# Decode attention over 65,536 keys: whole key tiles at the head, two value tiles in one run of TensorE's loop, and another order of the last pieces

## The chip, the cores and the metric

The kernel runs on one core of a Trainium2 chip. The metric is device time in microseconds (us), the median of repeated executions. A profile is one further execution, recorded by the hardware profiler: it has a time of its own, and a span from the first to the last recorded instruction. All times inside the profile count from the start of that span.

## What is computed

One decode step of attention with grouped heads: 32 query heads share 8 key/value heads, so each of the 8 groups has 4 queries, 65,536 keys and as many values of 128 numbers, in bf16.

```python
B, Hq, Hkv, Sq, Sk, D = 1, 32, 8, 1, 65536, 128
scores = jnp.einsum("bhqd,bhkd->bhqk", q, k) * scale     # k, v repeated 4 times over heads
p = _softmax(scores, axis=-1)
return jnp.einsum("bhqk,bhkd->bhqd", p, v)
```

Keys and values are 16 MiB for each group, 268.4 MB for the eight groups together. Each byte is read once.

## The kernel before

**Tiles.** A tile is half of one group's keys or values: 256 rows in each of 128 partitions, 64 KB a partition, 8 MiB in all. A tile is called k or v with its group and half: k00 is the first half of the keys of group 0, v71 the second half of the values of group 7. The on-chip buffer `buf` is a ring of three tiles. SyncE issues all loads on one queue, in a fixed order: k00, k01, k10, k11, v00, then for each group g from 2 to 7 the tiles kg0, kg1, v(g-2)1, v(g-1)0, and at the end v61, v70, v71 (line 153). With more than three tiles, the load of a tile waits until the tile three places earlier in the list has been used, because it goes into the same place of the ring (lines 158 to 169). For k10, k20, and the first halves of keys in general, that is told by `clr`, the count of cleared score banks: the place of a first half of keys is free once the third bank of its group has been cleared, since the first two banks are then done. The place of a second half of keys is free by `kb`, which VectorE raises when the group's four banks are closed. The place of a value tile is free by `vit`, raised by TensorE after every 32 rows.

So the load of k11 (fourth in the list) waits for the third bank of group 0, that of v00 for `kb` of group 0, that of k20 (sixth) for the third bank of group 1, that of k21 for `kb` of group 1, and that of v01 for the values v00.

**Landing.** A load raises its semaphore by 16 when all of it has landed. The tiles of group 0, and those of the last key group, are loaded as two transfers of 128 rows; their halves have the semaphores `sK[b][0]` and `sK[b][1]` of the ring's place b. The key tiles between are one transfer that raises `sK[b][0]` alone; for them ScalarE raises `sK[b][1]` ahead of time with three counts, in the first turn of its loop (lines 254 to 258). The value tiles v60, v61 and v70 are loaded in parts (`BY`), v71 in eight pieces (`PIECES`, of 64, 64, 32, 32, 44, 8, 8 and 4 rows).

**Keys.** VectorE transposes a landed half tile in place, one instruction of 128x8192 words (`turn`, line 312), and raises `kt`. For each half tile TensorE clears a score bank (`clr`), runs 32 matmuls into it and closes it (blocks "bank" to "bank_end"). A group has four half tiles and four banks. Then VectorE takes the maximum, TensorE spreads it ("summed"), ScalarE takes the exponentials of all four banks, and VectorE transposes the weights (`weights`).

**Values.** TensorE's block "values" handles 32 rows a turn, 8 matmuls, once `sV` says that they have landed; for the last four value tiles GpSimd passes the landings on to `sV` (lines 215 to 220). `r_w` is the column of the weights, `r_e` where the run ends. A run ends in "values_done", from where TensorE goes on to "turn" (the next group's keys, or "late", which sets the end of the next run), to "summed" or to "tail". In groups 0 to 7 a run is one value tile. VectorE's `picked` reduces a finished sum, TensorE's `chosen` gathers it.

**The end.** In block "tail" TensorE multiplies the piece of 44 rows with 11 matmuls, closes the bank, multiplies the last 8, 8 and 4 rows one by one into another bank, waits for VectorE's `picked` (`mxs`), adds it by `chosen`, and ScalarE scales and stores the result.

The lines that the prediction's steps touch most:

```python
140    first = load(0, kr[0], 0, 0, NT // 2)
164                sp.wait_ge(*((kb, wh + 1) if ws else (clr, 4 * wh + 3)))
314        for x in range(2):
315            take(dve, sK[b][x], 16)
318            dve.transpose(out=kv, in_=kv).then_inc(kt, 1)
450        take(pe, kt)
451        clear(sc[:, ds(value(r_x, 4) * 512, 512)]).then_inc(clr, 1)
```

Of the kernel before, what the change touches and what calls it, by code (L numbers as in the profile page):

```python
# [9 lines left out]
ALU = mybir.AluOpType  # L10
# [3 lines left out]
G = 8  # L14
H = 4
P = 128
D = 128
NT = 256
# [1 line left out]
C = 16  # L20
SLIDE = P + 4 * (W - 1)
BY = {
    (G - 2, 0): (128, 128), (G - 2, 1): (128, 128), (G - 1, 0): (128, 64, 64),
}
N = 2
FAR = 2.0 ** 126
STEP = 32
PIECES = (64, 64, 32, 32, 44, 8, 8, 4)
MOVED = 4


# [1 line left out]
def kernel(  # L33
# [18 lines left out]
    _, Hkv, Sk, _ = k.shape  # L52
# [5 lines left out]
    pe, dve, act, pool, sp = nc.tensor, nc.vector, nc.scalar, nc.gpsimd, nc.sync  # L58
# [16 lines left out]
    o_r = sbuf("o_r", (P, D + 3))  # L75
# [6 lines left out]
    sel = sbuf("sel", (P, H))  # L82
# [9 lines left out]
    misc = psum("misc", (P, 512))  # L92
# [7 lines left out]
    sK = [[sem(f"sK{b}{x}") for x in range(2)] for b in range(3)]  # L100
# [11 lines left out]
    wqs = sem("wqs")  # L112
    cst = sem("cst")
    mxs = sem("mxs")
# [5 lines left out]
    outs = sem("outs")  # L120
    rls = sem("rls")
    end = sem("end")
    dl = sem("dl")
    pl = sem("pl")
    cleared = list(sems)
# [3 lines left out]
    kr = [k[0, g].rearrange("(p n) d -> p (n d)", p=P) for g in range(G)]  # L129
    vr = [v[0, g].rearrange("(p n) d -> p (n d)", p=P) for g in range(G)]  # L130

    def load(at, src, s, lo=0, n=NT):
        at = at % 3 * half + lo * D
        return sp.dma_start(  # L134
            out=buf[:, at:at + n * D], in_=src[:, s * half + lo * D:s * half + (lo + n) * D]
        )

    first = load(0, kr[0], 0, 0, NT // 2)  # L140
    tc.no_tile_sem_insts.add(first.ins.name)
    first.then_inc(sK[0][0], 16)
    tc.add_to_no_dep_group("first", first.ins)
# [3 lines left out]
    tc.compile()  # L147


    load(0, kr[0], 0, NT // 2, NT // 2).then_inc(sK[0][1], 16)  # L150
    load(1, kr[0], 1, 0, NT // 2).then_inc(sK[1][0], 16)
    load(1, kr[0], 1, NT // 2, NT // 2).then_inc(sK[1][1], 16)
    tiles = [("k", 0, 0), ("k", 0, 1), ("k", 1, 0), ("k", 1, 1), ("v", 0, 0)]
    for g in range(2, G):
        tiles += [("k", g, 0), ("k", g, 1), ("v", g - 2, 1), ("v", g - 1, 0)]
# [2 lines left out]
    for at, (kind, h, s) in enumerate(tiles):  # L158
        if at < 2:
            continue  # L160
        if at > 2:
            was, wh, ws = tiles[at - 3]
            if was == "k":
                sp.wait_ge(*((kb, wh + 1) if ws else (clr, 4 * wh + 3)))
            else:

                if (wh, ws) not in BY:
                    sp.wait_ge((sC, sD)[ws], 16 * (wh + 1)).then_inc(sV, NT // STEP)
                sp.wait_ge(vit, NT // STEP * (2 * wh + ws + 1))
        if kind == "k" and h == G - 1:  # L170
            for x in range(2):
                load(at, kr[h], s, x * NT // 2, NT // 2).then_inc(sK[at % 3][x], 16)
        elif kind == "k":
            load(at, kr[h], s).then_inc(sK[at % 3][0], 16)
        elif (h, s) == (G - 1, 1):
            lo = 0
            for n, land in zip(PIECES, sP):
                load(at, vr[h], s, lo, n).then_inc(land, 16)
                lo += n
        elif (h, s) in BY:  # L180
            lo = 0
            for n in BY[h, s]:
                load(at, vr[h], s, lo, n).then_inc(lands.pop(0), 16)
                lo += n
        else:
            load(at, vr[h], s).then_inc((sC, sD)[s], 16)
# [7 lines left out]
        out=ident[:, :], in_=ident[:, :], compare_op=ALU.not_equal, fill=1.0,  # L194
# [8 lines left out]
    for g in range(G):  # L203
        if g == 0:
            pool.wait_ge(qxs, 1)
        else:
            pool.wait_ge(outs, g)
        pool.tensor_tensor(  # L208
            out=wv[:, :, :, 0:H],
# [6 lines left out]
    for at, (land, n) in enumerate(list(zip(sL, sum(BY.values(), ()))) + list(zip(sP, PIECES))[:MOVED]):  # L216

        pool.wait_ge(land, 32 if land is sP[0] else 16).then_inc(sV, n // STEP)
        if at + 1 == len(BY[G - 2, 0]):
            pool.wait_ge(outs, G).then_inc(wqs, 2)  # L220

    def take(engine, semaphore, n=1):

        engine.wait_ge(semaphore, n).then_inc(semaphore, -n)  # L224


    act.dma_start(out=qn, in_=q[0, :, 0, :]).then_inc(sQ, 16)
    act.wait_ge(qps, 1)
    act.copy(
        out=qx[:, :].rearrange("p (b r h) -> p b h r", b=2, r=2),  # L230
# [10 lines left out]
    for g in range(G + 1):  # L241
        if g < G:
            act.wait_ge(nms, g + 1)
            act.activation(  # L244
                out=E[:, :], in_=sc[:, :], func=ACT.Exp, bias=nmb[:, 0:1], scale=SCALE,
                accum_out=o_r[:, D:D + 1],
            ).then_inc(exd, 1)

        act.wait_ge(rls, g + 1)
        at = max(g - 1, 0) * D  # L250
        act.activation(  # L251
            out=o_out[:, at:at + D], in_=psum_f[0:H, 0:D], func=ACT.Copy, scale=rl
        ).then_inc(outs, 1)
        if g == 0:

            for b in range(3):
                n = sum(kind == "k" and at % 3 == b and 0 < h < G - 1 for at, (kind, h, _) in enumerate(tiles))
                act.nop().then_inc(sK[b][1], 16 * n)
    act.wait_ge(outs, G + 1)
    store(1, 0, G - 1)  # L260
    act.wait_ge(end, 1)
# [1 line left out]
        out=o_out[:, 0:D], in_=misc[0:H, 0:D], func=ACT.Copy, scale=rl_next  # L263
# [18 lines left out]
    def select(out, pattern, **at):  # L282
# [7 lines left out]
        out=rep.rearrange("p (a x) -> p a x", a=4),  # L290
# [7 lines left out]
        out=rows4[:, :].rearrange("k (y d) -> k y d", y=4),  # L298
# [4 lines left out]
        out=away.rearrange("k (q z r h) -> k z q r h", q=4, z=2, r=4)[:, 0],  # L303
# [5 lines left out]
        out=qt.bitcast(fp32), in_=qn.bitcast(fp32)  # L309
# [25 lines left out]
    def over():  # L335

        dve.reciprocal(out=rl_next, in_=psum_f[0:H, D:D + 1]).then_inc(rls, 1)  # L337
# [5 lines left out]
    block = block_of(dve)  # L343
    r_h, r_k = dve.alloc_register("h"), dve.alloc_register("k")
    h, kb_at = value(r_h, G + 1), value(r_k, 3)
# [19 lines left out]
    with block("turned"):  # L365
# [8 lines left out]
            out=same[:, :].rearrange("p (x h) -> p x h", h=H),  # L374
# [11 lines left out]
    with block("last"):  # L386
        dve.wait_ge(exd, 1)
        dve.wait_ge(vit, NT // STEP * (2 * G - 3))
        weights(0)
        dve.wait_ge(vdone, 1)  # L390
        next_over().then_inc(mxs, 1)
        picked().then_inc(mxs, 1)
        weights(1).then_inc(sP[0], 16)
        dve.wait_ge(pes, 2)
        over()
        dve.wait_ge(vdone, 2)
        picked().then_inc(mxs, 1)

        for _ in range(11):
            dve.nop().then_inc(dl, 1)  # L400
        dve.nop().then_inc(fin, 1)
        dve.br("done")
# [9 lines left out]
    block = block_of(pe)  # L412

    def add(reg, n, op=ALU.add):
        pe.reg_alu(reg, reg, n, op)
# [10 lines left out]

        return 4 * (row // W * W + W - 1 - row % W)

    def chosen(out, start, n=D):

        return pe.matmul(out=out[0:H, 0:n], lhsT=sel[:, :], rhs=o_r[:, 0:n], start=start, stop=True)  # L431

    r_g, g = counter("g", G + 2)
    r_x, x = counter("x", 6)
# [65 lines left out]
    with block("summed"):  # L500
        close(psum_o[:, :]).then_inc(vdone, 1)
        take(pe, mxs)

        pe.matmul(  # L504
            out=misc[:, :], lhsT=same[:, :], rhs=each[:, :].unsqueeze(1).broadcast_to([P, 16, 32]),
            start=True, stop=True,
        ).then_inc(pes, 1)
        take(pe, mxs)
        clear(psum_o[:, :], away, rows4[:, :])
        pe.reg_mov(r_x, 5)  # L510
        chosen(psum_f, True, D + 1).then_inc(pes, 1)
        add(r_g, 1)
        pe.br_ne(g, 1, on_true="values", on_false="turn")
    with block("turn"):
        take(pe, wqs)
        pe.reg_mov(r_x, 0)
        pe.br_lt(g, G, on_true="bank", on_false="late")
    with block("late"):

        pe.reg_alu(r_e, r_g, 4 * (sum(PIECES[:MOVED]) - NT), ALU.mult)  # L520
        add(r_e, 2048 - 4 * G * (sum(PIECES[:MOVED]) - NT))
        pe.br("values")

    with block("tail"):
        at = sum(PIECES[:MOVED])
        left = list(zip(PIECES, sP))[MOVED:]
        own = (2 * G * 2 - 1) % 3 * half
        final = 1024
        for n, land in left[:1]:
            pe.wait_ge(land, 16)  # L530
            for row in range(at, at + n, 4):
                qd = row // 4 % 4 * 32
                pe.matmul(  # L533
                    out=psum_o[qd:qd + 16, :], lhsT=Ew[:, final + column(row + 3):][:, 0:16],
                    rhs=buf[:, own + row * D:own + (row + 4) * D], start=False, stop=False,
                )
            at += n
        close(psum_o[:, :]).then_inc(vdone, 1)
        for y, (n, land) in enumerate(left[1:]):
            pe.wait_ge(land, 16)  # L540
            for row in range(at, at + n):
                pe.matmul(  # L542
                    out=misc[0:H, 0:D], lhsT=Ew[:, final + column(row):][:, 0:H],
                    rhs=buf[:, own + row * D:own + (row + 1) * D],
                    start=(row == at and y == 0), stop=False,
                )
            at += n
        pe.wait_ge(mxs, 1)
        chosen(misc, False).then_inc(end, 1)
        pe.br("done")  # L550
    nc.switch_bb("done", parent=home)

# [35 lines left out]
```

## Time and profile before

| | |
|---|---|
| median of 3 runs | 628.53 us (628.41 to 628.55) |
| the profiled execution's own time | 628.39 us |
| its span, first to last instruction | 626.5 us |
| mean granted TensorE clock | 0.929 |
| bytes read | 268.44 MB, 429 GB/s over the span |
| busy: TensorE, VectorE, ScalarE, GpSimd | 504.5, 331.4, 21.1, 6.0 us |

How the rows are read. In a timeline a row gives the start, the time taken, the engine (PE is TensorE, PEld its weight loads, DVE VectorE, ACT ScalarE, SPq SyncE's queue of issues), the line of the kernel, the operation, what it writes and reads, the count, and in brackets how long the engine was idle before it and what released it. A row of one line's instructions with the word "landing" gives the time from the issue of a transfer until it had landed (smallest, median, largest). A row of windows gives a stretch, its length, the busy time and the number of instructions of each engine, the granted TensorE clock as a share of full speed, the share of DMA time and GB/s. In the chain of waits each row is a start, a duration and what the end of the execution hung on. A transfer's landing time is its issue plus its time to landing.

### The profile page before, as it was taken

The page shows a single profiled execution, that of the slowest core. Times are in us where ns is not written, and L with a number is a line of the kernel's source. Part 1 is how long each engine was busy: PE and PEld are TensorE (multiplying, and loading weights), DVE is VectorE, ACT ScalarE, POOL GpSimd, SP SyncE. Part 2 cuts the span into 40 slices and gives each one's busy share as a digit, 9 for nine tenths or more (in the row PEclk, how much of TensorE's full clock was granted, in tenths as well). Part 3 has the DMA queues.
Part 4 walks back from the last instruction along what each step waited for, and adds up shares of the span by engine and source line. Part 5 has one row for each costly group of instructions (what it writes and reads, how often), then busy time and mean ns, then how long its engine had stood idle before and what let it go on. Part 6 is the DMA issues. An engine that isn't in the chain of part 4 may idle for free. (4 is left out here: it accounts for less than half of the span.)

```text
span 626.5 us, 8015 instructions
## 1 busy us (share of the span) xinstructions
PE 504.5 (81%) x2186; PEld 204.2 (33%) x2186; DVE 331.4 (53%) x109; ACT 21.1 (3%) x28; POOL 6.0 (1%) x16
## 2 busy tenths in 40 slices
PE   0587299798994889948799397993979988799997
PEld 0232043243331333313333133331433333333333
DVE  3983895789214892148821588215872389410100
ACT  1000100100010000100001000010000100001000
POOL 2000000000000000000000000000000000000000
PEclk9998589799998789988899889997899998999999
DMA  9999999999999999999999999999999999999997
GB/s 371 433 469 402 469 402 469 402 460 410 452 418 423 448 402 469 402 469 402 469 402 469 402 469 402 469 402 469 402 464 406 418 425 429 435 435 435 423 431 319
DMA packets 6857, 268.46 MB, mean 429 GB/s; under 512 B 840, under 2 KB 968, under 8 KB 1224
## 3 DMA queue, kind: packets, MB, share of 16 engines
q1 hardware_dynamic: 6768, 268.44, 99.4%
q10 hardware_dynamic: 88, 0.02, 0.0%
q14 instruction: 1, 0.01, 0.0%
HBM read 268.44 MB, written 0.01 MB: 429 GB/s over the span
## 5 line engine op out<-in xcount | busy, mean ns | idle before, releaser
L318 DVE STREAM_TRANSPOSE buf<-buf 128x8192 f32<-128x8192 f32 x32 | 277.2, 8694 | 87.2 <-DVEq L224 87.2
L460 PE MATMUL sc<-buf,zeros 128*128 x1024 | 247.8, 401 | 0.0
L484 PE MATMUL psum_o<-buf,Ew 128*16 x1008 | 226.0, 382 | 11.7 <-PEq L224 11.0
L460 PEld LDWEIGHTS sc<-buf,zeros 128*128 x1024 | 102.3, 100 | 137.7 <-issue 41.6
L484 PEld LDWEIGHTS psum_o<-buf,Ew 128*16 x1008 | 89.3, 89 | 145.2 <-issue 54.9
L418 PE MATMUL sc<-zeros 128*128 128x512 bf16 x32 | 13.8, 432 | 87.8 <-PEq L224 87.8
L331 DVE TENSOR_REDUCE o_r<-psum_o 128x128 f32<-128x512 f32 x10 | 6.9, 688 | 100.2 <-DVEq L224 72.4
L327 DVE COPY o_r<-o_r 4x1 f32<-4x1 f32 x9 | 1.3, 142 | 79.7 <-DVEq L224 65.6
L418 PEld LDWEIGHTS sc<-zeros 128*128 128x128 bf16 x32 | 3.1, 98 | 97.1 <-issue 96.0
L244 ACT ACTIVATE zeros<-sc,nmb 128x2048 bf16<-128x2048 f32 x8 | 15.7, 1967 | 535.9 <-DVE nmb L382 535.9
L323 DVE STREAM_TRANSPOSE Ew<-zeros 128x1024 bf16<-128x1024 bf16 x18 | 22.3, 1240 | 14.0 <-PE psum_o L484 14.0
L504 PE MATMUL misc<-each,same 128*128 128x512 f32 x18 | 11.3, 712 | 8.6 <-PEq L224 8.6
L370 DVE TENSOR_REDUCE mx<-sc 128x1 f32<-128x2048 f32 x8 | 18.0, 2253 | 0.0
L441 PE MATMUL misc<-Ew 32*128 32x128 bf16 x1 | 0.3, 283 | 10.7 <-DVE Ew L308 10.7
L208 POOL TENSOR_TENSOR zeros<-qx,quad 128x64 bf16<-128x64 bf16 x8 | 2.4, 294 | 486.6 <-ACT o_out L251 480.4
L504 PEld LDWEIGHTS misc<-each,same 128*128 128x128 f32 x18 | 2.9, 202 | 8.9 <-issue 8.8
L421 PE MATMUL sc<-zeros 128*128 128x1 bf16 x32 | 5.2, 163 | 0.0
L418 PE MATMUL psum_o<-rows,zeros 4*128 4x512 bf16 x10 | 4.5, 451 | 0.0
L289 DVE CAST Ew<-ident 32x128 bf16<-32x128 f32 x1 | 3.0, 2984 | 2.7 <-POOL ident L193 2.7
L421 PEld LDWEIGHTS sc<-zeros 128*128 128x128 bf16 x32 | 3.0, 95 | 3.9
L251 ACT ACTIVATE o_out<-psum_f,o_r 4x128 bf16<-4x128 f32 x9 | 3.1, 345 | 29.3 <-DVE o_r L337 29.3
L431 PE MATMUL psum_f<-o_r,sel 128*4 128x129 f32 x18 | 3.9, 302 | 0.0
(32 smaller groups left out, 31.9 us busy)
## 6 DMA issues: line engine op xcount, KB each, us to landing
buf<-in_k_dram SPq DMA_DIRECT2D x8, 4096.0 KB, 28.5
buf<-in_v_dram SPq DMA_DIRECT2D x5, 4096.0 KB, 32.5
buf<-in_v_dram SPq DMA_DIRECT2D x4, 2048.0 KB, 36.4
buf<-in_v_dram SPq DMA_DIRECT2D x2, 1024.0 KB, 38.7
buf<-in_v_dram SPq DMA_DIRECT2D x1, 1408.0 KB, 42.6
buf<-in_v_dram SPq DMA_DIRECT2D x2, 256.0 KB, 40.6
buf<-in_k_dram SPq DMA_DIRECT2D x12, 34.6
buf<-in_v_dram SPq DMA_DIRECT2D x12, 34.4
```

The lines of the kernel that those rows point to most:

```text
L244: act.activation(out=E[:, :], in_=sc[:, :], func=ACT.Exp, bias=nmb[:, 0:1], scale=SCALE, accum_out=o_r[:, D:D + 1],).then_inc(exd, 1)
L251: act.activation(out=o_out[:, at:at + D], in_=psum_f[0:H, 0:D], func=ACT.Copy, scale=rl).then_inc(outs, 1)
L318: dve.transpose(out=kv, in_=kv).then_inc(kt, 1)
L323: return dve.transpose(out=Ew[:, at], in_=E[:, at])
L331: return dve.tensor_reduce(out=o_r[:, 0:D], in_=psum_o[:, :].rearrange("p (y d) -> p d y", y=4), axis=AX.X, op=ALU.max)
L370: after(dve.tensor_reduce(out=mx[:, :], in_=sc[:, :], axis=AX.X, op=ALU.max))
L418: return pe.matmul(out=bank, lhsT=lhsT, rhs=rhs, start=True, stop=False)
L421: return pe.matmul(out=bank[:, 0:1], lhsT=zer[:, 0:P], rhs=zer[:, 0:1], start=False, stop=True)
L431: return pe.matmul(out=out[0:H, 0:n], lhsT=sel[:, :], rhs=o_r[:, 0:n], start=start, stop=True)
L460: pe.matmul(out=bank, lhsT=moved(wq[:, m * SLIDE + 4 * n:][:, 0:P], slide), rhs=moved(T[:, n, m // 2, m % 2], keys), start=False, stop=False,)
L484: last = pe.matmul(out=psum_o[0:16, :], lhsT=moved(Ew[:, column(4 * j + 3):][:, 0:16], weight), rhs=moved(buf[:, 4 * j * D:][:, 0:4 * D], ...
L504: pe.matmul(out=misc[:, :], lhsT=same[:, :], rhs=each[:, :].unsqueeze(1).broadcast_to([P, 16, 32]), start=True, stop=True,).then_inc(pes, 1)
```

## The change

- The tiles k00, k01 and k70 are loaded as one transfer each, where they were two; k71 stays two. The three counts that ScalarE gives for whole key tiles stand now at the start of its program, and count the tiles of group 0 and k70 too.
- v60 is one transfer (it was two), v70 two of 128 rows (it was 128, 64, 64). v61 stays two.
- TensorE's end of a value run for the last two groups is set in block "summed", ahead of the clear, so that v60 and v61 are one run of the loop, and v70 and the first 192 rows of v71 another. The way over "values_done", "turn" and "late" between the two tiles falls away, and with it GpSimd's two counts on `wqs`.
- The last pieces are 44, 9, 7 and 4 rows; TensorE waits for `picked` and issues `chosen` ahead of the last 4 rows, and the last row's matmul ends the sum.
- Of VectorE's eleven counts behind the last `picked`, six stand ahead of its wait for the bank of 44 rows.

```diff
@@
-    (G - 2, 0): (128, 128), (G - 2, 1): (128, 128), (G - 1, 0): (128, 64, 64),
+    (G - 2, 0): (NT,), (G - 2, 1): (128, 128), (G - 1, 0): (128, 128),
@@
-PIECES = (64, 64, 32, 32, 44, 8, 8, 4)
+PIECES = (64, 64, 32, 32, 44, 9, 7, 4)
@@
-    first = load(0, kr[0], 0, 0, NT // 2)
+    first = load(0, kr[0], 0)
@@
-    load(0, kr[0], 0, NT // 2, NT // 2).then_inc(sK[0][1], 16)
-    load(1, kr[0], 1, 0, NT // 2).then_inc(sK[1][0], 16)
-    load(1, kr[0], 1, NT // 2, NT // 2).then_inc(sK[1][1], 16)
+    load(1, kr[0], 1).then_inc(sK[1][0], 16)
@@
-        if kind == "k" and h == G - 1:
+        if (kind, h, s) == ("k", G - 1, 1):
@@
-            pool.wait_ge(outs, G).then_inc(wqs, 2)
+            pool.wait_ge(outs, G)
@@
     act.dma_start(out=qn, in_=q[0, :, 0, :]).then_inc(sQ, 16)
+
+    for b in range(3):
+        n = sum(kind == "k" and at % 3 == b and (h, s) != (G - 1, 1) for at, (kind, h, s) in enumerate(tiles))
+        act.nop().then_inc(sK[b][1], 16 * n)
@@
-        if g == 0:
-
-            for b in range(3):
-                n = sum(kind == "k" and at % 3 == b and 0 < h < G - 1 for at, (kind, h, _) in enumerate(tiles))
-                act.nop().then_inc(sK[b][1], 16 * n)
@@
         over()
+        for _ in range(6):
+            dve.nop().then_inc(dl, 1)
         dve.wait_ge(vdone, 2)
         picked().then_inc(mxs, 1)
-
-        for _ in range(11):
+        for _ in range(5):
             dve.nop().then_inc(dl, 1)
@@
+        add(r_g, 1)
+        pe.br_lt(g, G, on_true="first", on_false="late")
+    with block("late"):
+        pe.reg_alu(r_e, r_g, 4 * (sum(PIECES[:MOVED]) - NT), ALU.mult)
+        add(r_e, 2048 - 4 * G * (sum(PIECES[:MOVED]) - NT))
+        pe.br("cleared")
+    with block("first"):
+        pe.reg_mov(r_x, 5)
+        pe.br("cleared")
+    with block("cleared"):
         take(pe, mxs)
         clear(psum_o[:, :], away, rows4[:, :])
-        pe.reg_mov(r_x, 5)
         chosen(psum_f, True, D + 1).then_inc(pes, 1)
-        add(r_g, 1)
         pe.br_ne(g, 1, on_true="values", on_false="turn")
     with block("turn"):
         take(pe, wqs)
         pe.reg_mov(r_x, 0)
-        pe.br_lt(g, G, on_true="bank", on_false="late")
-    with block("late"):
...
+        pe.br("bank")
@@
         for y, (n, land) in enumerate(left[1:]):
+            if y == len(left) - 2:
+                pe.wait_ge(mxs, 1)
+                chosen(misc, False, stop=False)
             pe.wait_ge(land, 16)
...
-        pe.wait_ge(mxs, 1)
-        chosen(misc, False).then_inc(end, 1)
+        last.then_inc(end, 1)
```

More of the change, by code (lines that the diff above doesn't have):

```diff
@@ L427, in column, with chosen @@
         return 4 * (row // W * W + W - 1 - row % W)
-    def chosen(out, start, n=D):
-        return pe.matmul(out=out[0:H, 0:n], lhsT=sel[:, :], rhs=o_r[:, 0:n], start=start, stop=True)
+    def chosen(out, start, n=D, stop=True):
+        return pe.matmul(out=out[0:H, 0:n], lhsT=sel[:, :], rhs=o_r[:, 0:n], start=start, stop=stop)
     r_g, g = counter("g", G + 2)
@@ L516 @@
         pe.reg_mov(r_x, 0)
-        pe.br_lt(g, G, on_true="bank", on_false="late")
-    with block("late"):
-        pe.reg_alu(r_e, r_g, 4 * (sum(PIECES[:MOVED]) - NT), ALU.mult)
-        add(r_e, 2048 - 4 * G * (sum(PIECES[:MOVED]) - NT))
-        pe.br("values")
+        pe.br("bank")
     with block("tail"):
@@ L539 @@
         for y, (n, land) in enumerate(left[1:]):
+            if y == len(left) - 2:
+                pe.wait_ge(mxs, 1)
+                chosen(misc, False, stop=False)
             pe.wait_ge(land, 16)
             for row in range(at, at + n):
-                pe.matmul(
+                last = pe.matmul(
                     out=misc[0:H, 0:D], lhsT=Ew[:, final + column(row):][:, 0:H],
                     rhs=buf[:, own + row * D:own + (row + 1) * D],
-                    start=(row == at and y == 0), stop=False,
+                    start=(row == at and y == 0), stop=row == NT - 1,
                 )
             at += n
-        pe.wait_ge(mxs, 1)
-        chosen(misc, False).then_inc(end, 1)
+        last.then_inc(end, 1)
         pe.br("done")
```

## The prediction

> **What bounds the kernel now.** I read the page first, for the DMA rows, and then the chain of waits.
>
> ```profile
> DMA  9999999999999999999999999999999999999997
> q1 hardware_dynamic: 6768, 268.44, 99.4%
> ```
> ```profile
> 579.43 42.63 DMA buf<-in_v_dram
> 622.06 0.04 issue
> 622.10 0.82 PE psum_o L533 x11
> ...
> 623.03 1.27 PE misc L542 x20
> 624.31 0.23 PE misc L431 x2
> ```
>
> The queue of loads is busy from end to end, and the chain ends on a landing (622.06) with 2.5 us of TensorE behind it and then the store. So the time is the stream of 268 MB plus any hole in it. An edit on an engine is worth something only where it opens or closes a hole, or behind the last pieces. The next view is therefore SyncE's: when each load is issued and lands.
>
> ```profile
> 0.74 0.37 SPq L134 DMA_DIRECT2D buf<-in_k_dram  x1
> ...
> DMA to landing us min/median/max: 12.2/12.2/12.2
> ...
> L134 SPq DMA_DIRECT2D buf<-in_k_dram x3: 328/428/492, 1.9 to 2.8; - x3
> ...
> DMA to landing us min/median/max: 20.7/30.0/39.2
> ```
> ```profile
> 60.62 0.33 SPq L134 DMA_DIRECT2D buf<-in_v_dram  x1
> ...
> DMA to landing us min/median/max: 39.7/39.7/39.7
> ```
> ```profile
> 94.87 0.33 SPq L134 DMA_DIRECT2D buf<-in_k_dram  x1
> ...
> DMA to landing us min/median/max: 24.8/24.8/24.8
> ```
>
> The first half of k00 lands at 0.74 + 12.2 = 12.94; the next three halves follow, at 22.6 (1.9 + 20.7) and so on to 42.0 (2.8 + 39.2), so a half takes (42.0 − 12.94)/3 = 9.69. The tile v00 lands at 60.62 + 39.7 = 100.32 and k20 behind it at 94.87 + 24.8 = 119.67: a whole tile takes 19.35. From an empty queue the first half needed 12.2 where the stream needs 9.7, so a load that finds the queue empty pays **2.5 us** more. To leave no hole, k20 must be issued by 100.32 − 2.5 = 97.8. It is issued at 94.87. This is the number to watch: **2.95 us of slack**, at a load that waits for the third score bank of group 1.
>
> **The start, which decides.** With k00 and k01 as single transfers, VectorE's first transpose waits for 8 MiB instead of 4.
>
> ```profile
> 10.37 0.23 DVE L308 STREAM_TRANSPOSE Ew<-Ew 32x64 f32<-32x64 f32 x1 [4.36 <-DMA Ew<-in_q_dram]
> 13.04 8.71 DVE L318 STREAM_TRANSPOSE buf<-buf 128x8192 f32<-128x8192 f32 x1 [2.43 <-DVEq L224]
> 22.74 8.71 DVE L318 STREAM_TRANSPOSE buf<-buf 128x8192 f32<-128x8192 f32 x1 [0.99 <-DVEq L224]
> 32.45 8.71 DVE L318 STREAM_TRANSPOSE buf<-buf 128x8192 f32<-128x8192 f32 x1 [1.00 <-DVEq L224]
> 42.16 8.71 DVE L318 STREAM_TRANSPOSE buf<-buf 128x8192 f32<-128x8192 f32 x1 [1.00 <-DVEq L224]
> 60.45 0.14 DVE L327 COPY o_r<-o_r 4x1 f32<-4x1 f32 x1 [9.58 <-DVEq L224]
> ...
> 68.26 34.49 DVE L318 STREAM_TRANSPOSE buf<-buf 128x8192 f32<-128x8192 f32 x4 [0.64 <-DVEq L224]
> ```
> ```profile
> 22.44 9.64 PE L460 MATMUL sc<-buf,zeros 128*128 x32
> ...
> 41.46 0.39 PE L418 MATMUL sc<-zeros 128*128 128x512 bf16 x1 [2.17 <-PEq L224]
> ...
> 48.78 0.16 PE L421 MATMUL sc<-zeros 128*128 128x1 bf16 x1
> 51.17 0.39 PE L418 MATMUL sc<-zeros 128*128 128x512 bf16 x1 [2.22 <-PEq L224]
> ...
> 60.14 0.16 PE L421 MATMUL sc<-zeros 128*128 128x1 bf16 x1
> ```
> ```profile
> 94.45 0.39 PE L418 MATMUL sc<-zeros 128*128 128x512 bf16 x1 [0.24 <-PEq L224]
> ```
>
> Before, each of the four transposes starts 0.1 behind its half's landing. Where all data are there, four take 34.49, 8.62 each. A bank is cleared 0.30 behind its transpose's end (32.45 + 8.71 = 41.16, then 41.46) and takes 7.48 from clear to close (41.46 to 48.94), or 9.13 in the slow case (51.17 to 60.30).
>
> Afterwards: k00 lands whole at 22.6; transposes 1 and 2 run 22.7 to 39.95. k01 lands at 42.0; 3 and 4 run 42.1 to 59.35. Banks 1 and 2 run from 31.65 to about 49.2 (0.4, the first's 9.64, then 7.5). Bank 3 is cleared at 50.75 + 0.30 = 51.05 and bank 4 at 59.65, or when bank 3 is done if that is later. Bank 4 so closes at 67.15 if all runs at 7.5; at 67.7 if bank 3 takes 9.1 (then 60.2 + 7.5); at 68.8 if bank 4 does. Before it closed at 60.30: a delay of **6.85, 7.4 or 8.5**.
>
> ```profile
> 51.50:55.00 3.50, 3.50 (x10) 1.30 (x10) 0.00 (x0) 0.00 (x0) 0.00 (x0) 0.52 0.69 300
> ```
>
> Which one hangs on the granted clock: it was 0.52 in the first 3.5 us of the slow bank, behind an idle 2.2, and yet the bank before it, behind an idle 2.2 too, took 7.48. Ahead of bank 3 TensorE will be idle for 1.9, ahead of bank 4 for 1.1 or nothing, so I take the middle of the first two, 7.1. The Trainium skill, "TensorE: Matmul & The Clock Gate", Part 1, says that the gate goes by activity in windows of about 3.4 us which run free of the program. The two equal idles with different ends agree with it; by that rule the choice among the three delays changes from run to run, and the sum below with it by up to 1.4.
>
> From bank 4 on, the work between (60.45 to 68.26, four transposes back to back, 94.45) has no landing in it that comes late: k10 lands at 42.0 + 19.35 = 61.4 and k11 one tile later, at 80.7, where their transposes now start at 75.4 and 92.6. k11 itself is issued at 51.5 instead of 41.9, needed by 58.9. So the third bank of group 1 moves by the whole 7.1, and k20 is issued at 94.87 + 7.1 = 101.97. That is past 97.8 by 4.15: **a hole of 4.15 us in the stream** (3.9 to 5.6 by the three delays; 1.65 if restarting an empty queue cost nothing, which no row supports, and never a gain). A hole isn't made good later, as the stream is the bound.
>
> The Trainium skill, "DMA: Bandwidth & Descriptors", Anatomy of one DMA, fits a fixed 2.0 us and the bytes at 436 GB/s to one transfer, on another issue path. By it the hole would be an estimated 3.65; the row's 2.5 is taken.
>
> **Does the next load make a second hole?**
>
> ```profile
> 110.86 0.33 SPq L134 DMA_DIRECT2D buf<-in_k_dram  x1
> ...
> DMA to landing us min/median/max: 28.1/28.1/28.1
> ```
> ```profile
> 132.74 0.33 SPq L134 DMA_DIRECT2D buf<-in_v_dram  x1
> ...
> DMA to landing us min/median/max: 25.6/25.6/25.6
> ```
>
> k20 will land at 123.8. k21, issued at 118.0, is needed by 121.3: enough. It lands at 143.2, so v01 must be issued by 140.7; it was issued at 132.74, which becomes 139.8, as it waits for v00's matmuls, behind the same chain. 0.8 are left whatever the delay is. From there on slack grows: a group's four tiles take 77 us of stream, and 58 of TensorE (four banks of 7.5, two runs of 14.2).
>
> **Fewer, larger transfers.** Five pairs become one. Two halves take 2 × 9.69 = 19.38 against 19.35: 0.03 a pair, within the rows' rounding (0 to 0.1). Two pairs lie ahead of the hole and are lost in it; three give −0.1 (0 to −0.3).
>
> **The end of the stream.** Here the times of before are used; all move by the hole alike.
>
> ```profile
> 526.31 8.71 DVE L318 STREAM_TRANSPOSE buf<-buf 128x8192 f32<-128x8192 f32 x1 [1.00 <-DVEq L224]
> ```
> ```profile
> 545.86 15.66 PE L484 MATMUL psum_o<-buf,Ew 128*16 x64 [3.04 <-PEq L224]
> ...
> 563.41 14.19 PE L484 MATMUL psum_o<-buf,Ew 128*16 x64
> 578.65 14.21 PE L484 MATMUL psum_o<-buf,Ew 128*16 x64 [1.05 <-PEq L224]
> ...
> 594.94 14.05 PE L484 MATMUL psum_o<-buf,Ew 128*16 x64
> 610.01 3.71 PE L484 MATMUL psum_o<-buf,Ew 128*16 x16 [1.01 <-PEq L224]
> ...
> 622.10 0.82 PE L533 MATMUL psum_o<-buf,Ew 128*16 128x512 bf16 x11 [0.94 <-DMA buf<-in_v_dram]
> ```
>
> The last key group's transposes ended at 526.31 + 8.71 = 535.0. With k70 whole the first starts one half later, and the four run back to back from 506.9 (526.31 less two of 9.71): to 541.4, 6.4 later. Bank 4 then closes at 541.7 + 7.5 = 549.2, and v51 starts 1.0 behind, at 550.2. It was started by its landing at 545.86, on a slow clock; behind busy banks it takes 14.2, to 564.4. v60 follows at 566.3 (1.9 later, as from 561.5 to 563.4). The 44 rows end at 622.06, 236 of 256 rows into v71, so v70 lands at about 622.06 − 17.84 = 604.2 and v60 at 565.5 (estimates): v60 isn't late as a whole tile. v60 and v61 without the idle 1.05 take 28.4, to 594.7, and v70 starts at 596.7 (2.0 later, as from 592.9 to 594.9). Its second half is needed at 603.7 but lands at 604.2, and 0.3 pass on the way by GpSimd, so it ends at 604.5 + 7.0 = 611.5, and six steps of 1.75 follow without the idle 1.01, to 622.0. Where TensorE waited 0.94 for the 44 rows it comes up with them: +0.2 (0 to +0.9, the cost if its queue needs the whole of that wait to reach block "tail").
>
> `chosen` ahead of the last 4 rows leaves the count of matmuls as it was, and the rows' 1.27 and its 0.23 only change places: −0.1 (−0.23 if all of it is hidden; +0.2 if it waits for `picked`). Taken at nothing: ScalarE's counts (idle until TensorE has spread q); VectorE's six counts (in its wait of some 28 us; 0.2 if not); and q's load, which now shares the engines with larger packets: twice as late it would let VectorE go on at 21, ahead of 22.6.
>
> **The sum**, against the profiled execution's 628.39 (0.14 under the median): + 4.15 − 0.1 + 0.2 − 0.1 = **632.5 us**; with all bounds at their near ends 631.8 (3.9 − 0.3 + 0 − 0.23), at their far ends 635.1 (5.6 + 0 + 0.9 + 0.2), which needs the slowest of the three delays.
>
> **Rivals.**
> (a) *The slack takes the delay*; not slower. If group 1's third bank comes less than 2.95 late, there is no hole, and the time is 628.39 − 0.2 + 0.1 = 628.3. For it: TensorE and VectorE idle much of the first 70 us. Against it: each step from 22.6 to 94.87 waits for the one before, at spacings that the rows give, and the shortest delay is 6.85.
> (b) *A second hole* at v01: one slow stretch of TensorE (9.13 − 7.48 = 1.65) takes its 0.8 and leaves 0.9: 633.4. For it, group 1's weights and v00 run behind idle TensorE; against it, before they did so too.
> (c) *TensorE ends last.* If its way to the tail costs the full 0.9 and the run of v70 another 0.3: 633.5. For it the 0.94 shrinking to nothing; against it, the loop runs without the two turns.
> (d) *Fewer transfers pay.* The same page of the Trainium skill, Bandwidth, advises batching, and a fixed price for each transfer would make it so; here all transfers are far above its 1 MiB. With 2.5 for each of five transfers fewer, 12.5 less: 616. Against it, halves land 9.69 apart in a queue that is never empty.
>
> **How the numbers follow.** The forecast (one hole of some 4 us) has 0.78, (a) 0.09, (b) 0.07, (c) 0.04, (d) 0.02. This kernel's measurement tells 0.2% (1.3 us) from nothing. Slower: forecast, (b) and (c), 0.89; same: (a), 0.09; faster: (d), 0.02. The range, 631.0 to 634.8, holds the forecast's bounds but for the last 0.3, (b) and (c), and below them 0.8 for a cheaper restart of the queue; it leaves out (a), (d) and those tails.
>
> **What would show it.** Right: the first transpose at 22.7, group 0's fourth bank closing at 67 to 69, k20 issued at 101 to 103, the DMA row with a slice below 9 there, k20 landing at 123 to 126 and everything behind it 4 later; TensorE's wait ahead of the 44 rows under 0.5. Wrong: a stream with no hole at 100, or k20 issued before 97.8; a second hole; an end that moves by more than the hole.

## The result, and the profile after

The changed kernel takes 632.3 us (632.08 to 632.61, 6 runs) against 628.24 for the kernel before (627.76 to 628.55, 6 runs): a ratio of 1.0067, interval 1.0056 to 1.0077. That is slower by 4.06 us. The profiled execution took 632.08, with a span of 630.2.

First the page of the changed kernel, its rows on the DMA queue:

```profile
DMA  9999997999999999999999999999999999999998
GB/s 400 420 445 437 428 441 291 453 412 466 399 466 399 466 399 466 399 466 399 466 399 466 399 466 399 466 399 466 399 466 408 458 403 462 412 453 406 433 427 333
q1 hardware_dynamic: 6048, 268.44, 98.8%
```

The share of the queue fell from 99.4% to 98.8% of the span, and one of the 40 slices stands out: the seventh, 94.5 to 110.3 us, with a 7 and 291 GB/s. SyncE's rows and the landings, for the loads of v00, k20 and v01 in this order:

```profile
67.50 0.33 SPq L134 DMA_DIRECT2D buf<-in_v_dram  x1
...
DMA to landing us min/median/max: 32.5/32.5/32.5
```
```profile
102.25 0.33 SPq L134 DMA_DIRECT2D buf<-in_k_dram  x1
...
DMA to landing us min/median/max: 21.8/21.8/21.8
```
```profile
140.68 0.33 SPq L134 DMA_DIRECT2D buf<-in_v_dram  x1
```

v00 lands at 67.50 + 32.5 = 100.0. k20 is issued 2.25 after that and lands at 102.25 + 21.8 = 124.05, 4.4 later than before (119.67). The interval between the two landings is 24.05 instead of 19.35: a hole of 4.7, of which 0.3 is the earlier landing of v00. Of k20's 21.8, 19.35 is the tile's own time and **2.45** the restart of an empty queue, close to the 2.5 that the first load of the kernel before had given. The fit of 2.0 in the Trainium skill ("DMA: Bandwidth & Descriptors", Anatomy of one DMA), made on another issue path, is 0.45 short of it.

Why k20 came late stands in the timeline of VectorE, and that of TensorE's clears and closes, of the first two groups:

```profile
12.92 0.23 DVE L305 STREAM_TRANSPOSE Ew<-Ew 32x64 f32<-32x64 f32 x1 [6.91 <-DMA Ew<-in_q_dram]
22.73 17.30 DVE L315 STREAM_TRANSPOSE buf<-buf 128x8192 f32<-128x8192 f32 x2 [9.58 <-DVEq L222]
42.06 17.30 DVE L315 STREAM_TRANSPOSE buf<-buf 128x8192 f32<-128x8192 f32 x2 [2.02 <-DVEq L222]
67.34 0.14 DVE L324 COPY o_r<-o_r 4x1 f32<-4x1 f32 x1 [7.97 <-DVEq L222]
...
75.64 34.49 DVE L315 STREAM_TRANSPOSE buf<-buf 128x8192 f32<-128x8192 f32 x4 [0.64 <-DVEq L222]
```
```profile
51.07 0.39 PE L418 MATMUL sc<-zeros 128*128 128x512 bf16 x1 [2.67 <-PEq L222]
...
59.66 0.39 PE L418 MATMUL sc<-zeros 128*128 128x512 bf16 x1 [1.09 <-PEq L222]
...
67.02 0.16 PE L421 MATMUL sc<-zeros 128*128 128x1 bf16 x1
...
71.49 2.05 PE L504 MATMUL misc<-each,same 128*128 128x512 f32 x2 [4.01 <-PEq L222]
...
101.84 0.39 PE L418 MATMUL sc<-zeros 128*128 128x512 bf16 x1 [1.06 <-PEq L222]
```

The four transposes end at 59.36 instead of 50.87, bank 4 closes at 67.18 instead of 60.30, group 1's transposes start at 75.64 instead of 68.26, and its third bank is cleared at 101.84 instead of 94.45. The delay of 6.9 grows to 7.4 between bank 4 and the next transposes: the two matmuls of "summed" took 2.05 at a granted clock of 0.50, where before they took 1.54 at 0.67. It is then handed on unchanged. The row of before:

```profile
64.61 1.54 PE L504 MATMUL misc<-each,same 128*128 128x512 f32 x2 [4.28 <-PEq L224]
```

Last the end: TensorE's value runs, and the chain of waits.

```profile
571.00 28.21 PE L484 MATMUL psum_o<-buf,Ew 128*16 x128
...
601.33 24.73 PE L484 MATMUL psum_o<-buf,Ew 128*16 x112
626.24 0.82 PE L537 MATMUL psum_o<-buf,Ew 128*16 128x512 bf16 x11 [0.18 <-DMA buf<-in_v_dram]
```
```profile
587.00 39.19 DMA buf<-in_v_dram
626.19 0.04 issue
626.24 0.82 PE psum_o L537 x11
...
627.17 0.98 PE misc L549 x16
628.15 0.22 PE misc L431 x2
628.37 0.24 PE misc L549 x4
628.61 0.02 issue
628.63 0.36 ACT o_out L259
```

Two value tiles are one run now, without the idle 1.05 and 1.01 between them. The run of v70 and v71 still ends ahead of the 44 rows' landing; TensorE waits 0.18 for it where it waited 0.94, so that landing sets the end as before. It comes at 626.19 instead of 622.06.

### The profile page after: what moved, and what is told of

Read it like the earlier page. It is cut to its first block, busy times and chain, and to the rows that moved or that the text cites. A ratio compares the mean times of both kernels' runs of the same rounds, so it can differ in the third digit from the quotient of the medians.

```text
span 630.2 us, 8000 instructions
## 1 busy us (share of the span) xinstructions
PE 498.1 (79%) x2186; PEld 202.9 (32%) x2186; DVE 330.7 (52%) x109; ACT 21.1 (3%) x28; POOL 6.0 (1%) x16
## 3 DMA queue, kind: packets, MB, share of 16 engines
q1 hardware_dynamic: 6048, 268.44, 98.8%
## 5 line engine op out<-in xcount | busy, mean ns | idle before, releaser
L460 PE MATMUL sc<-buf,zeros 128*128 x1024 | 243.0, 395 | 0.0
## 6 DMA issues: line engine op xcount, KB each, us to landing
buf<-in_k_dram SPq DMA_DIRECT2D x15, 32.5
```

Source lines behind the costliest of these rows:

```text
L460: pe.matmul(out=bank, lhsT=moved(wq[:, m * SLIDE + 4 * n:][:, 0:P], slide), rhs=moved(T[:, n, m // 2, m % 2], keys), start=False, stop=False,)
```

## The experiments

Four kernels tell apart which part of the change costs, four more what a delay costs and what the rest is worth. The theory is the prediction's: a late third bank in group 1 makes a hole ahead of k20. All differences are to the kernel before, timed beside them: 628.17 in the first four, 628.08 in the last four, which ran on another chip. Each profile is one execution.

**The start undone.**

```diff
 # from the changed kernel
-    first = load(0, kr[0], 0)
+    first = load(0, kr[0], 0, 0, NT // 2)
...
-    load(1, kr[0], 1).then_inc(sK[1][0], 16)
+    load(0, kr[0], 0, NT // 2, NT // 2).then_inc(sK[0][1], 16)
+    load(1, kr[0], 1, 0, NT // 2).then_inc(sK[1][0], 16)
+    load(1, kr[0], 1, NT // 2, NT // 2).then_inc(sK[1][1], 16)
```

ScalarE's counts, without those of group 0, stand in the first turn of its loop again.

> The changed kernel with k00 and k01 as two transfers each again, all else of the change kept. Theory (the hole ahead of k20 is the whole cost, made by the whole key tiles of group 0): no hole, k20 issued at about 94.9 and landing at 119.7, and the time 0 to 0.5 us under that of before. Rival (the end: whole v60 and v70 and the joined value runs hold TensorE): still 3 to 4 us over before.

627.84 us (10 runs), ratio 0.9994 (0.9984 to 1.0003). Its row for k20:

```profile
93.80 0.33 SPq L134 DMA_DIRECT2D buf<-in_k_dram  x1
...
DMA to landing us min/median/max: 26.0/26.0/26.0
```

k20 is issued at 93.8 and lands at 119.8: no hole, and no cost is left. So the joined runs, the whole v60, v70 and k70 and the new end do not hold the kernel up.

**The start alone.** The kernel before, with `first = load(0, kr[0], 0)`, `load(1, kr[0], 1)` and ScalarE's counts at its start.

> The kernel before with k00 and k01 as one transfer each and nothing else of the change. Theory: k20 issued 7 to 8 us later than before, at 102 to 103, a hole of 4.0 to 5.0, and the time 4.0 to 5.0 us over before, a little more than the changed kernel since the merged pairs behind the hole are missing. Rival (the end): no difference from before.

632.91 us (4 runs), ratio 1.0076 (1.0059 to 1.0092): 4.74 over before, and 0.6 more than the changed kernel. Its row for k20:

```profile
102.35 0.33 SPq L134 DMA_DIRECT2D buf<-in_k_dram  x1
...
DMA to landing us min/median/max: 21.8/21.8/21.8
```

The whole cost lies in the loads of k00 and k01.

**Only one of the two tiles whole.** The same edit for k00 alone, then for k01 alone, each with ScalarE's count for that tile's place of the ring at the start of its program.

```diff
 # k00 alone, from the kernel before
-    first = load(0, kr[0], 0, 0, NT // 2)
+    first = load(0, kr[0], 0)
-    load(0, kr[0], 0, NT // 2, NT // 2).then_inc(sK[0][1], 16)
 # k01 alone, from the kernel before
-    load(1, kr[0], 1, 0, NT // 2).then_inc(sK[1][0], 16)
-    load(1, kr[0], 1, NT // 2, NT // 2).then_inc(sK[1][1], 16)
+    load(1, kr[0], 1).then_inc(sK[1][0], 16)
```

> The kernel before with only k00 as one transfer. Theory: transposes 1 and 2 run 22.7 to 40.0, and 3 and 4 behind them without a pause to 57.2, since k01's halves have landed by then; bank 4 closes at about 65.0, 4.7 late; less the slack of 2.95 a hole of 1.75, so 1.5 to 2.1 us over before. Rival (the cost is the late start of the first transpose, 9.7 us): as much as the changed kernel, 4 us over.

> The kernel before with only k01 as one transfer. Theory: the first two transposes are as before, the third starts at 42.1 and the fourth ends at 59.35; bank 3 is cleared at 51.05 behind an idle of some 11 us, so on the slow clock, and bank 4 closes at 67.7 to 69.4, 7.4 to 9.1 late; a hole of 4.4 to 6.1 us, as much as with both tiles whole or more. Rival (the cost is the late start of the first transpose): no more than 1 us over before.

k00 alone: 630.64 us (7 runs), ratio 1.0039 (1.0026 to 1.0053), 2.5 over before; single runs from 629.68 to 632.7. k01 alone: 632.66 us (4 runs), ratio 1.0072 (1.0055 to 1.0089), 4.5 over before. The timeline of VectorE and the row of k20, first with k00 whole, then with k01 whole, and TensorE's third and fourth bank with k01 whole:

```profile
22.95 34.49 DVE L321 STREAM_TRANSPOSE buf<-buf 128x8192 f32<-128x8192 f32 x4 [9.58 <-DVEq L223]
```
```profile
100.34 0.33 SPq L134 DMA_DIRECT2D buf<-in_k_dram  x1
```
```profile
13.19 8.71 DVE L321 STREAM_TRANSPOSE buf<-buf 128x8192 f32<-128x8192 f32 x1 [2.66 <-DVEq L223]
22.89 8.71 DVE L321 STREAM_TRANSPOSE buf<-buf 128x8192 f32<-128x8192 f32 x1 [0.98 <-DVEq L223]
42.23 17.30 DVE L321 STREAM_TRANSPOSE buf<-buf 128x8192 f32<-128x8192 f32 x2 [10.63 <-DVEq L223]
```
```profile
102.55 0.33 SPq L134 DMA_DIRECT2D buf<-in_k_dram  x1
```
```profile
51.24 0.60 PE L421 MATMUL sc<-zeros 128*128 128x512 bf16 x1 [11.79 <-PEq L223]
51.63 8.80 PE L463 MATMUL sc<-buf,zeros 128*128 x32
60.27 0.16 PE L424 MATMUL sc<-zeros 128*128 128x1 bf16 x1
60.30 0.38 PE L421 MATMUL sc<-zeros 128*128 128x512 bf16 x1
...
67.47 0.16 PE L424 MATMUL sc<-zeros 128*128 128x1 bf16 x1
```

With k00 whole the first transpose is as late as in the changed kernel (22.95), but the four follow without a pause, end at 57.44 and win 1.9 back. With k01 whole the first is on time, and the cost is as high as with both: the third transpose starts at 42.2 with k01 whole and at 42.1 with both. Its third bank, behind an idle of 11.79, took 9.19 from clear to close, with a granted clock of 0.50 from 51.5 to 55.0; the fourth followed at once and closed at 67.63, 7.3 later than before. What counts is the end of the fourth, not the start of the first; the rival falls on both. The time with k00 whole lies 0.4 above the range that was written: k20's issue was 5.5 late, not 4.7, with a hole of 2.5 (100.34 + 21.8 − 100.3 − 19.35). Of the 5.5, 5.0 had come about by bank 4 (VectorE's next step at 65.42 for 60.45), and 0.5 came in the two matmuls of "summed", which took 2.05 here too. Whether the clock gate also spreads the runs is weighed below.

**A delay without any change of loads.** VectorE is given one or three reductions more, between group 0's last step and group 1's transposes.

```diff
+        dve.br_eq(h, 1, on_true="pad", on_false="next")
+    with block("pad"):
+        for i in range(3):
+            dve.tensor_reduce(
+                out=ident[:, 16 * i:16 * i + 16],
+                in_=same[:, :].unsqueeze(1).broadcast_to([P, 16, P]), axis=AX.X, op=ALU.max)
+        dve.br("next")
+    with block("next"):
```

> The kernel before with one reduction of 2048 words more on VectorE, of about 2.2 us, between group 0's last step and group 1's transposes; its result is not used. Theory (a delay there costs what it exceeds the slack of 2.95 by): k20 issued at about 97.1, no hole, no change of the time (within 0.5 us). Rival (any delay of the first groups costs its own length): 2.2 us over before.

> The same with three such reductions, 6.6 us, and all loads as before. Theory: k20 issued at about 101.5, a hole of 3.7, the time 3.2 to 4.5 us over before, as with the change. Rival (the cost of the change lies in the form of its loads, not in the delay): no change. Rival (any delay costs its own length): 6.6 us over.

One: 627.96 us (10 runs), ratio 0.9998 (0.9989 to 1.0008). Three: 629.98 us (10 runs, 628.84 to 631.37), ratio 1.0032 (1.0023 to 1.0041), 1.9 over before. The rows with three reductions: VectorE's start of group 0's last steps, the added work, the transposes; then v00 and k20.

```profile
58.83 0.14 DVE L327 COPY o_r<-o_r 4x1 f32<-4x1 f32 x1 [7.98 <-DVEq L224]
...
66.32 6.67 DVE L388 TENSOR_REDUCE ident<-same 128x16 f32<-128x2048 f32 x3
72.91 34.48 DVE L318 STREAM_TRANSPOSE buf<-buf 128x8192 f32<-128x8192 f32 x4
```
```profile
59.00 0.33 SPq L134 DMA_DIRECT2D buf<-in_v_dram  x1
...
DMA to landing us min/median/max: 41.4/41.4/41.4
```
```profile
99.51 0.33 SPq L134 DMA_DIRECT2D buf<-in_k_dram  x1
...
DMA to landing us min/median/max: 21.7/21.7/21.7
```

The threshold stands: with one reduction (2.29 long) k20 was issued at 95.32, under 97.8, and it cost nothing; with three it was issued at 99.51, past it, and cost by what it was past. So the runs place the threshold between 95.3 and 99.5. With one reduction the issue came 1.5 later than with the start undone (93.80), whose bank 4 ended at the same time. The size of the delay was over-estimated: bank 4 closed 1.6 earlier here than in the first profile (58.83 against 60.45 for VectorE's next step), as VectorE waited 7.98 for it instead of 9.58, and bank 4 ran at a granted clock of 1.00; and the reductions filled an idle 0.6. Against that, the two matmuls of "summed" took 0.4 longer (1.90 for 1.54). That 6.7 us of added work in the chain cost 1.9, and 2.3 cost nothing, is slack at work.

The rows of all ten profiles agree with the rule of the prediction: the hole is (issue of k20 + 2.45) less v00's landing, and nothing, within 0.1, while that is negative.

| kernel | k20 issued | v00 landed | issued + 2.45 − landed | measured hole |
|---|---|---|---|---|
| before | 94.87 | 100.3 | −3.0 | 0 |
| spare semaphores | 92.96 | 100.2 | −4.8 | −0.1 |
| start in halves, again | 93.70 | 100.0 | −3.8 | 0.1 |
| start in halves | 93.80 | 100.4 | −4.2 | 0 |
| one reduction | 95.32 | 100.2 | −2.4 | −0.1 |
| three reductions | 99.51 | 100.4 | 1.6 | 1.5 |
| k00 whole | 100.34 | 100.3 | 2.5 | 2.5 |
| changed | 102.25 | 100.0 | 4.7 | 4.7 |
| start alone | 102.35 | 100.0 | 4.8 | 4.8 |
| k01 whole | 102.55 | 100.2 | 4.8 | 4.8 |

(Measured: the interval of the two landings, each an issue plus its time to landing, less 19.35. The 2.45 is itself k20's 21.8 less 19.35, so the last two columns agree in the five rows with a hole wherever k20 needs 21.8. What these rows show is that it needs 21.7 or 21.8 in all five, however late it is issued, and more in the five without a hole, where it waits behind v00.)

**What the rest of the change is worth**, and a question on the end of the span. In the profiles of the kernel before, with the start alone, and with k00 or k01 whole, the span ended 1.9 us behind the start of ScalarE's last instruction (at 624.56 in the kernel before); in those of the changed kernel and of the one with its start undone 1.6 (from 628.63, and 624.44). The difference is in the landing of the last store, in front of which nothing else is left.

```diff
 # from the changed kernel with k00 and k01 in halves
+    for i in range(2):
+        sem(f"spare{i}")
     sS = sem("sS")
```

> The changed kernel with k00 and k01 in halves, and two semaphores more allocated and not used, so that the last store's semaphore has the number it has before. In the kernels with the old end one of the last store's four landings came some 0.37 us behind the other three, in those with the new end 0.04. Theory (the semaphore's number): late by 0.37 again, and 0.3 us over the same kernel without them. Rival (the new end itself): 0.04, and no difference.

> The changed kernel with k00 and k01 in halves once more, in more rounds. If the merged pairs behind the start and the new end are worth what the profiles show behind k20's landing (0.25 of stream and 0.4 from the 44 rows' landing to the end), 0.3 to 0.7 us under before; if the differences of single profiles are chance, no difference.

With the spare semaphores: 627.56 us (10 runs), ratio 0.9991 (0.9982 to 1.0001), and 1.6 from ScalarE's last instruction to the end: the semaphore's old number does not by itself make the landing late. Nor does the old end, since the kernels with one and with three reductions, which have both the old end and the old number, show 1.6 too. But these were profiled on the other chip, where all four kernels show 1.6, while on the first chip the three with the old end show 1.9 and the one with the new end 1.6. What delays the last landing stays open, the chip included. The kernel with its start in halves, again: 627.49 us (11 runs, 627.42 to 628.02; before 627.82 to 628.63 in 33), ratio 0.9991 (0.9982 to 1.0). Three series so lie 0.3 to 0.6 us under before, with intervals that reach 1 or just beyond: the changed kernel with its start in halves is the fastest tried, by a margin that these runs do not clearly tell from nothing.

## Why the prediction was right

**The bound and the threshold held.** The forecast of 632.5 was made for a profiled execution, which took 632.08; the median is 632.3. The cost came by the way that was described: the same load, the same queue, the delay less the slack. Undoing the start takes the cost away, the start alone brings it, and a delay with no change of loads brings it once it passes the threshold. That the total came so near is in part luck: k20 landed 4.4 later for 4.15, and the terms behind it came to −0.66 where they were to cancel to nothing, so two misses offset each other. The terms follow.

**The delay: 7.4 for 7.1.** Of the three cases the first occurred, 6.9 at bank 4. TensorE ran bank 3 in 7.5 (51.07 to 59.66, less the idle 1.09), so at a granted clock of 1.00, although it had been idle for 2.67 ahead of it, longer than the 2.2 behind which bank 4 was slow before. That agrees with the window that runs free of the program (the Trainium skill, "TensorE: Matmul & The Clock Gate", Part 1): idles of 2.2 and 2.7 do not decide by their length. The rest, 0.5, came behind bank 4, in the two matmuls of "summed" at the lower granted clock, a step that I had moved unchanged. The 7.1 was the middle of the first two cases. The first occurred, and a step that was not in the sum brought 0.5 more; that this comes so near to 7.1 is luck.

The base moves as well. VectorE's step behind bank 4 came at 60.45 in the profile of the kernel before, and between 58.79 and 58.91 in the five other profiles with group 0 in halves, which have no hole but for the one with three reductions. In the three of them without reductions k20 was issued between 92.96 and 93.80, so that against 97.8 the slack was 4.0 to 4.8 there; the 2.95 of the prediction is the least that was seen. This drops out of the forecast, which worked out both the old and the new time of k20 from one profile and so gave the time of its issue.

Where the slack is used up, such a shift should be in the time. The kernels just past the threshold do spread, over 2.5 us (three reductions) and 3.0 (k00 whole), the kernel before over 0.8 in 33 runs. But the kernels further past it spread less: the changed one over 0.5 in 6 runs, the start alone over 0.3 in 4 and k01 whole over 0.9 in 4. That the gate makes the spread is argued, not shown: it was not followed run by run, and why these three spread so little stays open.

**The restart: 2.45 for 2.5**: k20 needs 21.7 or 21.8 in each of the five profiles with a hole, less 19.35.

**The second hole did not open, narrowly.** v01 was issued at 140.68; by the landing of k21 (118.24 + 25.1 = 143.3) less 2.45 it was needed by 140.9. 0.2 were left of the 0.8 that I gave, as v00's matmuls ended 7.9 later than before (140.68 − 132.74), where the rest of the chain moved by 7.4: their run took 15.52 for 14.97. v01 landed at 162.8, 19.4 behind k21.

```profile
118.24 0.33 SPq L134 DMA_DIRECT2D buf<-in_k_dram  x1
...
DMA to landing us min/median/max: 25.1/25.1/25.1
```

**Merged pairs: −0.25 for −0.1.** From k20's landing to that of the 44 rows it was 502.4 before (622.06 − 119.67) and 502.1 after (626.19 − 124.05); within the bounds. It is 502.1 to 502.2 in all four profiles with the merged pairs and 502.4 to 502.9 in all six without, so the gain is real, and small: rival (d) had 2.5 for each pair. Its words that all transfers are far above 1 MiB do not hold for the last pieces (128 to 288 KB for the rows behind the 44), but none of those is among the merged pairs.

**The end.** The run of v70 and v71 ended a little ahead of the landing, where I had it come up with it. v70's second half, which I had landing 0.5 behind its need, landed at 608.0, some 0.4 ahead of it, and the run took 24.73 without a break. So of the +0.2 that I set for TensorE's way to the tail nothing came: the matmuls started 0.05 behind the landing as before. From the landing to ScalarE's start the new order takes 2.44 (628.63 − 626.19) against 2.50: −0.06 for −0.1; it is 2.43 to 2.45 in all four profiles with the new end and 2.48 to 2.51 in all six with the old. The store's last landing took 0.35 more off the profiled execution, which I had not in the sum at all.

So the profiled executions differ by +4.4 − 0.25 − 0.06 − 0.35 = 3.7 (632.08 − 628.39 = 3.69), the medians by 4.06.

**The costs at nothing held**: the query landed 2.6 later (VectorE went on at 12.92 for 10.37), far ahead of 22.73; neither ScalarE's counts nor VectorE's six show anywhere.

## What to carry to other kernels

In a kernel bound by its stream of loads, look for the load that is issued with the least time to spare, and follow back what releases it: a delay on that path cost nothing here up to that slack and, in the profiles, its full length beyond it, although VectorE was busy for only half of the span. Take the slack from more than one profile: here it was 2.95 in one and up to 4.8 in another. Larger first transfers put off the first use by half a tile, 9.7 us, and a merged pair gained under 0.1 us in a queue that was not empty; the place to merge transfers is behind the point where the slack has grown. Of several stages that each wait for a landing, the last one counted here, and a late first one was partly made good where later data were already there.

## What had not been expected of the hardware

The last store of 1 KB ended the span 1.9 us behind the start of ScalarE's last instruction in four profiles and 1.6 behind it in six. Neither the semaphore's number nor the order of the last pieces explains it alone, and the 0.35 between the two is more than the 0.06 that the new end gained. And the granted clock of one early bank moved a load by up to 1.7 us between profiles of kernels whose start is the same (v00 was issued at 60.62 in one and between 58.96 and 59.08 in five), with no hole in the five profiles that had slack left.
